# Four of nine token chunks in pairs with seven block products instead of eight (Strassen), weights from DRAM, and a cosine from one sine

## The chip, the cores and the metric

The kernel runs on one core of one Trainium2 chip. A core has five engines that run their own instruction streams side by side: PE (TensorE, matmuls), ACT (ScalarE), DVE (VectorE), POOL (GpSimd) and SP (SyncE), which here only issues DMA transfers. Engines wait for each other by semaphores. PE takes its operands from SBUF and writes into PSUM, which has eight banks of 512 fp32 columns; ACT and DVE read PSUM. The metric is the device time of one execution in microseconds, the median of the runs.

## What is computed

The reference, cut to its core (8 batches, 8 heads, 576 tokens, head size 64; 4608 tokens of width 512, inner width 2048):

```python
kv = np.einsum('bhsd,bhse->bhde', k, v)
out = np.einsum('bhsd,bhde->bhse', q, kv)
rms = np.sqrt(np.mean(out * out, axis=-1, keepdims=True) + 1e-06)
attn = out / rms * g_norm
x = attn.transpose(0, 2, 1, 3).reshape(B * S, H * D)   # 4608 x 512
h = x @ w_in                                           # first product, 512 x 2048
g = h * np.cos(h)
return (g @ w_out).astype(np.float32)                  # second product, 2048 x 512
```

## The kernel before

The 4608 tokens are cut into nine chunks of 512 (`CH`, `NCH`). For each chunk the attention part makes four tiles x of 128 features by 512 tokens (`NP` = 4, one tile for two heads). Then come 16 steps (`NJ`), one for each 128 of the inner width: the first product of step j adds four x tiles times a block of w_in into one PSUM bank (tile `bank`), `act_part` turns the bank into g = h cos h, and the second product (`stage2_part`) adds g times a block of w_out into four banks `acc`, one for each 128 tokens of the chunk.

Every fp32 operand is split into a high part in the matmul's own format (fp32r) and the rest (`xhi`/`xlo`, `ghi`/`glo`, and `w[:, 0]`/`w[:, 1]` of a weight). A product of two operands is three matmuls, high·high, low·high and high·low, so a step has 4 x 3 matmuls in the first product and as many in the second, all of 128 x 512.

`act_part` runs on ACT and DVE in turn: ki (ACT, the number of turns in h, rounded by the write to int32), r = h - ki C1 and r = r - ki C2 (DVE, twice), sine of r/2 and square (ACT, twice), (r - 0.5) h (DVE), then ghi (ACT) and glo (DVE). That makes g times -1/2, and the copy of `acc` to the output scales by -2.

`x_part` makes an x tile of chunks 2 to 8: DVE transposes q, ACT and DVE split it (`m`, `sg`), PE multiplies it with the split k-v product (`kv_w`) into two banks, ACT and DVE bring these together, then come square, transpose, reduce and a swap of rows (`part`, `swp`, `ms`), a power -1/2 on POOL (`rinv`), and the scaling with `gcol` (the norm's gain). x is last split into xhi and xlo. The attention of a chunk is done while an earlier chunk's steps run.

The weights arrive as 64-bit floats and are turned into split fp32 by `w_part` during the first two chunks; from then on all 32 blocks (`wi0` to `wi15`, `wo0` to `wo15`) stay in SBUF. At the start these same buffers hold k, v and q of the first two chunks.

The order of work on each engine is set by a planner in the kernel's Python code (`Order`): every part of the work is a generator that waits for events, takes buffer tokens (`t_bank` for PSUM banks, `t_slot`, `t_two`) and asks for time on an engine with a priority, mostly from `due(i)`, the time wanted for step i; a table of numbers (`haste`) moves single priorities. The instructions are pinned in the planned order, so on the chip each engine runs its own row, and waits where an input is late. All instructions are issued through one helper (line 207), so the profile's groups are told apart by tile names.

Of the kernel before, what the change touches and what calls it, by code (L numbers as in the profile page):

```python
# [19 lines left out]
P = 128  # L20
# [3 lines left out]

C1 = 6.28125
C2 = 2.0 * PI - C1

# [13 lines left out]
class Tokens:  # L41
    def __init__(self, n):
        self.free = [(0.0, i) for i in range(n)]
        self.waiters = []
# [7 lines left out]
class Order:  # L52
# [23 lines left out]
    def advance(self, proc, value):  # L76
        while True:
# [18 lines left out]
            else:  # L96
# [4 lines left out]
                t, value = heapq.heappop(tokens.free)  # L101
# [10 lines left out]
    def give(self, tokens, t, which=0):  # L112
        if tokens.waiters:
            _, _, proc = heapq.heappop(tokens.waiters)
            proc.t = max(proc.t, t)
            self.advance(proc, which)
        else:
            heapq.heappush(tokens.free, (t, which))
# [36 lines left out]
def tile_kernel(  # L155
# [73 lines left out]


# [24 lines left out]

    segments = [(0, 0, 4), (1, 0, 8), (0, 4, 16), (1, 8, 16)]
    segments += [(c, 0, NJ) for c in range(segments[-1][0] + 1, NCH)]
# [9 lines left out]
    STEP = 5.4  # L267

    def due(i):

        return 24.0 + STEP * i + 2.0 * min(i, 11)


    haste = {
# [9 lines left out]
        ("act", 16): 16.2, ("act", 29): 32.0, ("act", 35): 63.7, ("act", 4): -10, ("act", 5): -8.1,  # L284
        ("act", 8): 10.6, ("acc", 0): 28.7, ("acc", 1): 19.9, ("acc", 10): 20.7, ("acc", 13): 59.2,
        ("acc", 14): 44.4, ("acc", 18): 32.3, ("acc", 26): 10.6, ("acc", 28): 15.6, ("acc", 33): 25.2,
        ("acc", 46): 5.6, ("acc", 53): 6.8, ("acc", 8): 12.3, ("xd", 2, 0): -3.8, ("xd", 2, 2): -11.8,
        ("xd", 2, 3): -24.5, ("xd", 3, 0): -12.5,
# [50 lines left out]
    def load(us, prio, event, issue, wait=(), take=None):  # L339
        def part():  # L340
            if wait:
                yield "wait", wait
            if take:
                yield "take", take
# [6 lines left out]
    def load_g():  # L351
        pass
# [271 lines left out]
    def x_part(c, p, prio):  # L624
# [11 lines left out]
        for j, r in enumerate(rows):  # L636
            yield "run", [("ACT", act_us())], prio
            act.copy(out=qs[j][r], in_=qT[r])
            _, end = yield "run", dve_only(CH), prio
            dve.tensor_tensor(out=qs[j][rows[1 - j]], in0=qT[r], in1=qs[j][r].bitcast(F32), op=ALU.subtract)  # L640
# [16 lines left out]
        x_slot = yield "take", t_slot, prio  # L657
        x = slot_tile(x_slot)
# [39 lines left out]
        sched.give(t_slot, end, slot)  # L698
        yield "take", t_x, prio
# [58 lines left out]
    gates = [Event() for _ in steps]  # L758

    def window(c):  # L760

        first = last_step[c - 2] + 1
        return first, begin[c] - first

    def stage1_part(i):
# [3 lines left out]
        yield "wait", [w_done["wi", j]]  # L769
        yield "take", t_h  # L770
# [223 lines left out]
```

## Time and profile before

| what | value |
|---|---|
| median of 3 runs | 859.64 us (859.44 to 859.7) |
| profiled execution, first to last instruction (span) | 858.1 us |
| granted clock of PE, mean | 0.999 |
| instructions | 12178 |
| DMA | 59.51 MB, mean 69 GB/s |
| DMA in the first 60 us | 334 GB/s |

The span is what the profile covers; the device time of a run has a little more around it, 1.5 us by the median. In the rows of the profile an arrow reads "written tile <- read tiles", then come the shapes, "x" and the number of instructions, busy time in us, the mean of one in ns, and the time that the engine sat idle just before them with what ended it. PE's weight loads (PEld) overlap its matmuls. Rows of the timeline begin with the start in us and the length; rows of windows give a stretch and the busy time of each engine in it.

### The profile page before, as it was taken

The numbers are of one execution on the slowest core, as the hardware profiler recorded it, in microseconds if no ns is written. First come the engines' busy times: TensorE is split into PE (matmuls) and PEld (weight loads), VectorE is DVE, ScalarE is ACT, GpSimd is POOL, SyncE is SP. The second block draws the span as 40 slices with busy tenths as digits, with TensorE's granted clock in tenths as the row PEclk, the third lists the DMA queues.
The fourth block names the chain that finished last, engine by engine and source line by source line (L and its number), as shares of the span: only waits on it lengthen the run. The fifth ranks groups of instructions, "written<-read, shape, count | busy, mean of one in ns | idle before, by whom it ended". The sixth has DMA issues, their size and how long they took to land.

```text
span 858.1 us, 12178 instructions
## 1 busy us (share of the span) xinstructions
PE 848.1 (99%) x4496; PEld 701.5 (82%) x4496; DVE 651.0 (76%) x1053; ACT 556.2 (65%) x1059; POOL 103.6 (12%) x49
## 2 busy tenths in 40 slices
PE   8999999999999999999999999999999999999998
PEld 7678888888788888888888888888888888888886
DVE  4998988899987757885778667876777678864554
ACT  4888988666665656665666566756666666664443
POOL 3210000013121101110102101210112011110000
PEclk9999999999999999999999999999999999999999
DMA  9996021361304011301122020402000110010001
GB/s 306 323 321 216 2 86 37 101 194 33 104 15 116 5 63 24 111 12 39 45 66 63 3 73 13 121 4 62 13 13 14 49 25 1 2 45 4 1 1 49
DMA packets 104635, 59.51 MB, mean 69 GB/s; under 512 B 69632, under 2 KB 94976, under 8 KB 104576
## 3 DMA queue, kind: packets, MB, share of 16 engines
q1 hardware_dynamic: 104064, 58.02, 23.3%
q8 instruction: 35, 0.57, 0.3%
q10 hardware_dynamic: 512, 0.72, 0.2%
q14 instruction: 24, 0.20, 0.1%
HBM read 47.19 MB, written 11.53 MB: 68 GB/s over the span
## 4 chain that ended last, share of the span: by engine, by line
PE 95%; DVE 2%; POOL 1%; ACT 1%; DMA 1%; issue 0%; ACTq 0%; POOLq 0%; DVEq 0%
PE bank L207 49%; PE acc L207 45%; POOL rinv L207 1%; DVE r L207 1%; DMA gcol<-in_g_norm_dram 1%; DVE sg L207 0%; DVE ms L207 0%; ACT m L207 0%; ACT slot L207 0%; DVE xlo L207 0%; ACT r L207 0%; DVE m L207 0%; ACTq L207 0%; DVE wo L207 0%; ACT wo L207 0%
## 5 line engine op out<-in xcount | busy, mean ns | idle before, releaser
L207 PE MATMUL acc<-wo,ghi 128*128 128x512 f32 x1152 | 355.5, 390 | 0.0
L207 PE MATMUL bank<-xhi,wi 128*128 128x512 f32 x1088 | 337.1, 391 | 0.4 <-DVE wi L207 0.4
L207 PEld LDWEIGHTS acc<-wo,ghi 128*128 128x128 f32 x1152 | 215.6, 188 | 45.1 <-DVE slot L207 0.4
L207 ACT ACTIVATE r<-r 128x512 f32<-128x512 f32 x288 | 181.5, 631 | 94.6 <-DVE r L207 92.0
L207 PEld LDWEIGHTS bank<-xhi,wi 128*128 128x128 f32 x1088 | 202.4, 188 | 41.9 <-DVE wi L207 0.7
L207 PE MATMUL acc<-wo,glo 128*128 128x512 f32 x576 | 224.5, 390 | 0.3 <-DVE glo L207 0.3
L207 PE MATMUL bank<-xlo,wi 128*128 128x512 f32 x544 | 212.1, 390 | 0.1
L207 POOL TENSOR_TENSOR rinv<-ms,mhalf 128x16 f32<-128x16 f32 (+1 forms) x36 | 99.1, 2757 | 648.9 <-DVE ms L207 648.9
L207 DVE SCALAR_TENSOR_TENSOR r<-ki,bank 128x512 f32<-128x512 int32 x144 | 98.6, 685 | 72.3 <-ACT ki L207 70.8
L207 ACT ACTIVATE ki<-bank 128x512 int32<-128x512 f32 x144 | 85.6, 594 | 90.0 <-PE bank L207 86.4
L207 DVE SCALAR_TENSOR_TENSOR r<-r,bank 128x512 f32<-128x512 f32 x144 | 98.2, 682 | 55.1 <-ACT r L207 54.4
L207 PEld LDWEIGHTS acc<-wo,glo 128*128 128x128 f32 x576 | 108.1, 188 | 23.4 <-DVE glo L207 0.7
L207 PEld LDWEIGHTS bank<-xlo,wi 128*128 128x128 f32 x544 | 102.1, 188 | 21.9 <-DVE xlo L207 0.6
L207 ACT CAST ghi<-r 128x512 fp32r<-128x512 f32 x144 | 89.1, 620 | 43.5 <-DVE r L207 40.9
L207 DVE TENSOR_TENSOR glo<-r,ghi 128x512 fp32r<-128x512 f32 x144 | 98.9, 687 | 23.6 <-ACT ghi L207 21.3
L207 DVE SCALAR_TENSOR_TENSOR r<-ki,r 128x512 f32<-128x512 int32 x144 | 98.5, 684 | 1.2
L207 DVE TENSOR_TENSOR slot<-bank,slot 64x512 f32<-64x512 f32 x56 | 38.5, 688 | 19.1 <-ACT slot L207 18.1
L207 ACT COPY slot<-bank 64x512 f32<-64x512 f32 x56 | 32.5, 581 | 21.1 <-PE bank L207 20.2
L207 ACT ACTIVATE slot<-acc 128x512 f32<-128x512 f32 (+1 forms) x39 | 22.5, 592 | 9.6 <-PE acc L207 8.4
L207 ACT COPY swp<-part 32x16 f32<-32x16 f32 x112 | 22.6, 202 | 7.5 <-DVE part L207 5.8
L207 DVE STREAM_TRANSPOSE slot<-rinv 128x512 f32<-128x512 f32 x28 | 19.8, 705 | 4.1 <-POOL rinv L207 4.0
L207 DVE SCALAR_TENSOR_TENSOR sg<-sg,m 128x512 int32<-128x512 int32 x32 | 21.7, 685 | 0.3 <-ACT sg L207 0.3
(94 smaller groups left out, 573.3 us busy)
## 6 DMA issues: line engine op xcount, KB each, us to landing
out_dram<-slot SPq DMA_DIRECT2D x35, 256.0 KB, 2.0
wo<-in_moe_w_out_dram SPq DMA_DIRECT2D x16, 512.0 KB, 8.3
wi<-in_moe_w_in_dram SPq DMA_DIRECT2D x16, 512.0 KB, 9.4
m<-in_k_dram SPq DMA_DIRECT2D x24, 256.0 KB, 3.3
sg<-in_v_dram SPq DMA_DIRECT2D x24, 256.0 KB, 3.8
part<-slot SPq DMA_DIRECT2D x8, 256.0 KB, 5.3
slot<-part SPq DMA_DIRECT2D x8, 256.0 KB, 2.9
qb<-in_q_dram SPq DMA_DIRECT2D x32, 48.0 KB, 2.8
```

What stands on the lines that cost most here:

```text
L207: return lambda *a, **kw: tc.keep_in_program_order(f(*a, **kw))
```

## The change

**Seven products.** Chunks 0 to 4 (`PLAIN` = 5) keep their steps. Chunks 5 and 6, and 7 and 8, are taken as pairs. The x of a pair is seen as a 2 x 2 matrix of blocks (chunk by half of the features), and two blocks j = 2m, 2m+1 of w_in with their two halves as another. `quad_part` makes the four h tiles of a pair for two blocks in seven block products (A11, S1, S2, A12, S4, S3, A22; Strassen's scheme in Winograd's form) instead of eight. The sums of x (S1 to S4) are made by `cross_part` from the unsplit x tiles, and each of the seven operands is split anew; the sums of the weights are made once by `sums_part` on POOL and ACT during steps 40 to 79. Between products, ACT copies a bank to SBUF (`snap`), the next product adds on in the same bank, and DVE adds bank and copy (`add`).

**Weights from DRAM.** The split weights are written to DRAM (`keep_in`, `keep_out`, `sums_part`) from step 34 on, 56 pieces for the first product (`wq`) and 16 blocks for the second (`wod`). In the pairs they are loaded again, two pieces or one block of 512 KB at a time (`load_in` into buffers `wo8` to `wo11`, `load_out` into `wo12` to `wo15`). The other weight buffers become room for the seven operands (`wi0` to `wi13`), for copies (`wi14`, `wi15`) and for x and g tiles (`wo0` to `wo7`, and the former `xhi`, `xlo`, `r`).

**Second product.** In the pairs g is kept unsplit until `split_part` and `gather_part` take it, in units of one (chunk, j): 16 units of chunk 5 beside the first pair, 32 beside the second, the 16 of chunk 8 at the end.

**Cosine.** h comes out in turns, since 1/(2 pi) is put into `gcol`. Then cos h is the sine of 2 pi (h + 1/4 - round(h + 1/4)): ki (ACT), one subtraction (DVE), one sine (ACT), one product with h (DVE). The output is scaled by 2 pi.

**Engines and order.** Some additions and subtractions may go to POOL or DVE, whichever the planner finds free (`adders`). `haste` is another table, and `due` has another pace for the pairs.

The core of the diff:

```diff
-C1 = 6.28125
-C2 = 2.0 * PI - C1
+OUT_SCALE = 2.0 * PI
...
     def g_part():
         yield "wait", [g_in]
-        yield "run", [("ACT", 0.1)], -11.0
-        act.copy(out=gcol[D:2 * D, :], in_=gcol[0:D, :])
+        yield "run", [("ACT", 0.4)], -11.0
+        for r in (slice(D, 2 * D), slice(0, D)):
+            act.activation(out=gcol[r, :], in_=gcol[0:D, :], func=AF.Copy, scale=INV_2PI)
...
+    def adders(f=CH, late=0.4):
+        return [("POOL", 0.2 + f / 460, 0.0), ("DVE", dve_us(f), late)]
...
-        act.activation(out=ki, in_=h, func=AF.Copy, scale=INV_2PI)
+        act.activation(out=ki, in_=h, func=AF.Copy, bias=0.25)
...
-        dve.scalar_tensor_tensor(out=r, in0=ki, scalar=-C1, in1=h, op0=ALU.mult, op1=ALU.add)
+        dve.scalar_tensor_tensor(out=r, in0=h, scalar=0.25, in1=ki, op0=ALU.add, op1=ALU.subtract)
...
+        act.activation(out=r, in_=r, func=AF.Sin, scale=2.0 * PI)
-        dve.scalar_tensor_tensor(out=r, in0=ki, scalar=-C2, in1=r, op0=ALU.mult, op1=ALU.add)
-        act.activation(out=r, in_=r, func=AF.Sin, scale=0.5)
-        act.activation(out=r, in_=r, func=AF.Square)
-        dve.scalar_tensor_tensor(out=r, in0=r, scalar=0.5, in1=h, op0=ALU.subtract, op1=ALU.mult)
+        dve.tensor_tensor(out=r, in0=r, in1=h, op=ALU.mult)
...
+    def sums_part(m, prio):
+        yield "wait", [w_done["wi", 2 * m], w_done["wi", 2 * m + 1]]
...
+        for j, t in ((2 * m, even), (2 * m + 1, odd)):
+            w = w_split["wi", j].bitcast(F32)
+            pool.tensor_tensor(out=t, in0=w[:, 0], in1=w[:, 1], op=ALU.add)
...
+        pool.tensor_tensor(out=even, in0=odd, in1=even, op=ALU.subtract)
...
+        for t, places in ((even, (S1, A22)), (odd, (S3, S2))):
+            act.copy(out=hi, in_=t)
+            pool.tensor_tensor(out=t, in0=t, in1=hi.bitcast(F32), op=ALU.subtract)
+            for half, q in enumerate(places):
+                for n, part in enumerate((hi.bitcast(F32), t)):
+                    nc.sync.dma_start(out=wq[:, 7 * m + q, n], in_=part[:, half * WH:(half + 1) * WH])
...
+    def load_in():
+            slot = yield "take", t_win
+            w = wpool.tile([P, 2, 2, WH], F32R, name=f"wo{slot}")
+            nc.sync.dma_start(out=w.bitcast(F32), in_=wq[:, s:s + 2])
...
+        def product(q, bank, first, gate=None):
+            yield "wait", [win_in[s // 2]] + [cross_done[pair, q, k] for k in range(HK)]
+            for k in range(HK):
+                for i, (a, b) in enumerate(((0, 0), (1, 0), (0, 1))):
+                    pe.matmul(
+                        out=ps[bank], lhsT=w[:, s % 2, a, cols], rhs=x[:, b],
+                        start=(first and k == 0 and i == 0), stop=(k == HK - 1 and i == 2), skip_group_check=True)
...
+        end = yield from product(A11, b2, True, 0)
+        sched.spawn(snap("p1", b2, at(A11) - 8.0), end + 0.1)
+        end = yield from product(S1, b3, True)
+        sched.spawn(snap("p5", b3, at(S1) - 8.0), end + 0.1)
+        yield "wait", [done["p1"]]
+        end = yield from product(S2, b2, False, 1)
+        sched.spawn(snap("u2", b2, at(S2) - 8.0), end + 0.1)
+        end = yield from product(A12, b1, True)
+        yield "wait", [done["p5"]]
+        end = yield from product(S4, b3, False, 2)
+        yield "wait", [done["u2"]]
+        end = yield from product(S3, b2, False, 3)
+        yield "wait", [u3]
+        end = yield from product(A22, b2, False)
```

Three places in the order of instructions show what moved. Names carry a running number; a row stands for one instruction or, with "x3", for three alike.

On PE, at the entry into chunk 5, before: the last second products of chunk 4 (here that with `wo14`) are laced into the first step of chunk 5 (x times `wi0` into `bank3`):

```order
L207 MATMUL bank3_5098<-xhi_5070,wi0_448 128x512 x2
L207 MATMUL bank3_5098<-xlo_5071,wi0_448 128x512
L207 MATMUL acc0_4395<-wo14_1815,ghi_5153 128x512 x2
L207 MATMUL acc0_4395<-wo14_1815,glo_5154 128x512
L207 MATMUL acc1_4400<-wo14_1815,ghi_5153 128x512 x2
L207 MATMUL acc1_4400<-wo14_1815,glo_5154 128x512
L207 MATMUL acc2_4406<-wo14_1815,ghi_5153 128x512 x2
L207 MATMUL acc2_4406<-wo14_1815,glo_5154 128x512
L207 MATMUL acc3_4412<-wo14_1815,ghi_5153 128x512 x2
L207 MATMUL acc3_4412<-wo14_1815,glo_5154 128x512
```

On PE, the same entry now, from the last second product of chunk 4 (`wo15`): then come the products of the first quad, operands in `wi` buffers, weights in `wo8` to `wo10`; A11 stands further up in the row:

```order
L206 MATMUL acc3_4642<-wo15_1623,ghi_5416 128x512 x2
L206 MATMUL acc3_4642<-wo15_1623,glo_5417 128x512
L206 MATMUL bank0_5450<-wi2_5455,wo8_5254 128x512 x3
L206 MATMUL bank0_5450<-wi9_5564,wo8_5254 128x512 x3
L206 MATMUL bank3_5323<-wi4_5465,wo9_5318 128x512 x3
L206 MATMUL bank3_5323<-wi10_5576,wo9_5318 128x512 x3
L206 MATMUL bank1_5597<-wi3_5513,wo9_5318 128x512 x3
L206 MATMUL bank1_5597<-wi8_5584,wo9_5318 128x512 x3
L206 MATMUL bank0_5450<-wi5_5533,wo10_5344 128x512 x3
L206 MATMUL bank0_5450<-wi12_5604,wo10_5344 128x512 x3
L206 MATMUL bank3_5323<-wi6_5518,wo10_5344 128x512 x3
L206 MATMUL bank3_5323<-wi13_5598,wo10_5344 128x512 x3
```

S1, S2, A12, S4 and S3 follow each other without a second product between them, and `bank0` and `bank3` are each written a second time after two other products.

On ACT, the first instructions before (m and wo15 are parts of the attention of chunk 0, warm loads the sine's table):

```order
L207 DMA wi6_146<-in_k_dram 128x576
L207 DMA wo4_147<-in_v_dram 128x576
L207 ACT_TABLE_LOAD
L207 ACTIVATE warm_80<-warm_80 128x1
L207 DMA gcol_138<-in_g_norm_dram 64x1
L207 COPY gcol_138<-gcol_138 64x1
L207 COPY m_158<-bank0_152 128x512
L207 COPY m_169<-bank1_162 128x512
```

On ACT, the first instructions now:

```order
L206 ACT_TABLE_LOAD
L206 COPY m_177<-bank0_172 128x512
L206 DMA wi6_200<-in_k_dram 128x576
L206 DMA wo4_201<-in_v_dram 128x576
L206 ACT_TABLE_LOAD
L206 ACTIVATE warm_80<-warm_80 128x1
L206 DMA gcol_138<-in_g_norm_dram 64x1
L206 COPY wo15_158<-bank1_181 64x64 x2
L206 COPY wo15_158<-bank2_206 64x64 x2
L206 COPY m_243<-bank3_230 128x512
L206 ACTIVATE gcol_138<-gcol_138 64x1 x2
L206 ACTIVATE slot0_257<-acc3_245 128x512
```

The loads of k, v and g stand behind a copy that reads PE's first transpose, and a square (`slot0`) stands behind the two instructions on `gcol`.

On DVE, at the entry into chunk 5, before: the steps' instructions on r and the last splits (xlo, glo):

```order
L207 TENSOR_TENSOR xlo_5071<-slot1_4729,xhi_5070 128x512
L207 TENSOR_TENSOR xlo_5075<-slot0_4952,xhi_5074 128x512
L207 SCALAR_TENSOR_TENSOR r_5088<-ki_5055,bank2_4998 128x512
L207 SCALAR_TENSOR_TENSOR r_5088<-ki_5055,r_5088 128x512
L207 SCALAR_TENSOR_TENSOR r_5108<-ki_5102,bank0_5043 128x512
L207 SCALAR_TENSOR_TENSOR r_5088<-r_5088,bank2_4998 128x512
L207 SCALAR_TENSOR_TENSOR r_5108<-ki_5102,r_5108 128x512
L207 TENSOR_TENSOR glo_5154<-r_5088,ghi_5153 128x512
```

On DVE, the same entry now: the last x tile (`wo1`) is scaled between sums and splits of the products' operands (`slot3` and `slot4` are sums, `wi` their low parts):

```order
L206 STREAM_TRANSPOSE slot0_5515<-rinv_5451 128x512
L206 TENSOR_TENSOR wi3_5513<-xhi_4749,wi3_5513 128x512
L206 TENSOR_TENSOR wi6_5518<-wo0_4646,wi6_5518 128x512
L206 TENSOR_TENSOR wi7_5524<-wo1_4680,wi7_5524 128x512
L206 SCALAR_TENSOR_TENSOR wo1_4680<-wo1_4680,gcol_138,slot0_5515 128x512
L206 TENSOR_TENSOR kv_w_79<-bank2_5467,kv_w_79 64x4x64
L206 TENSOR_TENSOR slot3_5540<-wo0_4646,wo1_4680 128x512
L206 TENSOR_TENSOR sg_5464<-qT_5461,sg_5464 64x512
L206 TENSOR_TENSOR wi9_5564<-slot3_5540,wi9_5564 128x512
```

Between `rinv` and the operand of S1 (`wi9`) there are now nine instructions in DVE's row.

More of the change, by code (lines that the diff above doesn't have):

```diff
@@ new lines, in split_part @@
+    def split_part():
+        for u, (c, j) in enumerate(units):
+            prio = due_unit(u) - 4.0 + put_off("split", u)
+            yield "wait", [g_ready[c, j]]
+            yield "take", t_g, prio
+            r, held = g_raw[c, j]
+            yield "run", [("ACT", act_us())], prio
+            ghi = ew.tile([P, CH], F32R, name="ghi")
+            glo = ew.tile([P, CH], F32R, name="glo")
+            act.copy(out=ghi, in_=r)
+            e, end = yield "run", adders(CH, 0.0), prio
+            adder(e).tensor_tensor(out=glo, in0=r, in1=ghi.bitcast(F32), op=ALU.subtract)
+            sched.give(t_store, end, held)
+            g_pairs[c, j] = ghi, glo
+            sched.fire(g_split[c, j], end)
```

386 lines of the change are left out of this document (351 added, 35 removed), and 12 rows, old and new, of the table haste.

## The prediction

> **What bounds the kernel now.** I read the page first, then the groups with shapes kept apart, then a stretch of the timeline, then windows of one chunk each, and last the start of the timeline.
>
> ```profile
> span 858.1 us, 12178 instructions
> PE 848.1 (99%) x4496; PEld 701.5 (82%) x4496; DVE 651.0 (76%) x1053; ACT 556.2 (65%) x1059; POOL 103.6 (12%) x49
> PE 95%; DVE 2%; POOL 1%; ACT 1%; DMA 1%; issue 0%; ACTq 0%; POOLq 0%; DVEq 0%
> ```
>
> TensorE is busy in 99% of the span and is 95% of the chain that ended last. "Busy" is modelled, so I look at the rate:
>
> ```profile
> 606.40 0.61 PE L207 MATMUL acc<-wo,ghi 128*128 128x512 f32 x2
> 606.85 0.39 PE L207 MATMUL acc<-wo,glo 128*128 128x512 f32 x1
> 607.08 0.61 PE L207 MATMUL acc<-wo,ghi 128*128 128x512 f32 x2
> 607.53 0.39 PE L207 MATMUL acc<-wo,glo 128*128 128x512 f32 x1
> 607.76 0.61 PE L207 MATMUL acc<-wo,ghi 128*128 128x512 f32 x2
> ```
>
> Three matmuls start every 0.68 us (606.40, 607.08, 607.76): 0.2267 us each, whatever the listed 0.39. Now one chunk at a time, from one first product to the same one of the next chunk:
>
> ```profile
> 395.85:487.84 91.99, 91.99 (x482) 76.52 (x481) 68.56 (x110) 58.24 (x112) 11.92 (x4) 1.00 0.19 49
> 580.04:672.56 92.52, 92.52 (x481) 76.83 (x481) 68.95 (x110) 58.68 (x113) 11.91 (x4) 1.00 0.10 24
> ```
>
> The columns are length, busy time of PE, weight loads, DVE, ACT, POOL, then clock, DMA share and GB/s. 16 steps of 24 matmuls are 384 x 0.2267 = 87.0 us of the 92.0; the other 5.0 are the attention matmuls (8 of 512 columns, 1.8, and k-v products, some 3.1). There is no hole: DVE (75%) and ACT (63%) have reserve, and the clock is full. So in these chunks a matmul removed is 0.2267 us won, and DVE or ACT work removed is worth nothing by itself.
>
> **The products (the gain).** Per pair of chunks, eight quads of seven products replace 32 steps of first product. A product is 2 x 3 matmuls, a quad 42 instead of 48. Over 16 quads 96 matmuls go: 96 x 0.2267 = 21.8 us, all on the path that sets the end. The second product (1728 matmuls) and the attention matmuls stay. Weights are now taken from other buffers, still one load of 128 columns per matmul, so the rate stays. Against the span 858.1 this gives 836.3; the median of the runs, 859.64, lies 1.5 above the span, so 837.9 in device time.
>
> **The cosine.** Per tile one DVE and one ACT instruction go:
>
> ```profile
> L207 ACT ACTIVATE r<-r 128x512 f32<-128x512 f32 x288 | 181.5, 631 | 94.6 <-DVE r L207 92.0
> L207 DVE SCALAR_TENSOR_TENSOR r<-ki,bank 128x512 f32<-128x512 int32 x144 | 98.6, 685 | 72.3 <-ACT ki L207 70.8
> L207 DVE SCALAR_TENSOR_TENSOR r<-ki,r 128x512 f32<-128x512 int32 x144 | 98.5, 684 | 1.2
> L207 DVE TENSOR_TENSOR glo<-r,ghi 128x512 fp32r<-128x512 f32 x144 | 98.9, 687 | 23.6 <-ACT ghi L207 21.3
> ```
>
> That is 144 x 0.684 = 98.5 us of DVE and 144 x 0.631 = 90.9 us of ACT. Both lie beside TensorE: gain zero on the path, but it is what pays for the rest.
>
> **What is added.** DVE: 48 additions that finish the products and 28 more sums and splits of x, less 37 that the order puts on POOL: 105 fewer in all. ACT: 48 copies out of PSUM, 12 more splits, 16 casts of weight sums: 68 fewer in all. POOL: 64 instructions for the weight sums and those 37. They cost nothing on the path as long as each stage has room, so I count the fullest one. Between the first product of the first pair and the first of the second, the order has 551 matmuls, about 118 us at the rates above, 174 instructions on DVE and 178 on ACT: it holds the attention of chunks 7 and 8 too. At the page's means (651.0/1053 = 0.618 and 556.2/1059 = 0.525, overlaps included) DVE takes 107.5 us, 91%, and ACT 93, 79%. At the 0.685 of a full tile DVE would take 119, that is 101%. So here the cover is thin, though units of second product are in store for PE. Bounds 0 and 12 us; I take 1.5, near the lower end, since the 0.618 includes the mix.
>
> POOL has not yet done such work. Its nearest rows:
>
> ```profile
> masks.py:199 POOL TENSOR_SCALAR_AFFINE_SELECT ident<-ident 128x128 f32<-128x128 f32 x1 | 0.3, 292 | 0.1
> masks.py:197 POOL MEMSET ident<- 128x128 f32 x1 | 0.2, 199 | 0.0
> L207 POOL MEMSET kv_w<- 128x1024 f32 x2 | 1.8, 951 | 0.0
> ```
>
> A write alone costs 0.84 ns a column (752 ns over 896 columns) and 0.09 us fixed; one read and a write 1.6 ns. A sum of two tiles of 512 columns then lies between 0.5 and some 1.8 us; I take 1.2, above the row with one read. The pow rows (2.90 us for 16 columns, below) are a function per element and no price for a subtraction. The weight sums are 8 x (5 x 1.2 + 3 x 0.65) = 64 us on a POOL that was idle for 80 of every 92 us.
>
> **Entry into a pair.** The order puts the last attention matmuls of chunk 6 inside the last step of chunk 4; the product with S1 needs what follows from them. The chain from there is made of these rows:
>
> ```profile
> L207 ACT COPY slot<-bank 64x512 f32<-64x512 f32 x56 | 32.5, 581 | 21.1 <-PE bank L207 20.2
> L207 DVE TENSOR_TENSOR slot<-bank,slot 64x512 f32<-64x512 f32 x56 | 38.5, 688 | 19.1 <-ACT slot L207 18.1
> L207 ACT ACTIVATE slot<-slot 128x512 f32<-128x512 f32 x28 | 17.6, 628 | 4.6 <-DVE slot L207 4.0
> L207 DVE STREAM_TRANSPOSE qT<-slot 128x512 f32<-128x512 f32 x28 | 19.8, 706 | 0.9 <-ACT slot L207 0.7
> L207 DVE TENSOR_REDUCE part<-qT 128x16 f32<-128x512 f32 x28 | 19.0, 677 | 0.4
> L207 ACT COPY swp<-part 32x16 f32<-32x16 f32 x112 | 22.6, 202 | 7.5 <-DVE part L207 5.8
> L207 DVE SCALAR_TENSOR_TENSOR ms<-part,swp 128x16 f32<-128x16 f32 x28 | 4.8, 170 | 4.1 <-ACT swp L207 4.0
> ```
>
> Two evacuations 2 x (0.58 + 0.69), square 0.63, transpose and reduce 1.38, four swaps 0.81, 0.17, pow some 3.1 (rows below), five DVE instructions of the order 3.5, then sum, cast and subtraction with one more DVE instruction between 2.5: 14.6, with hand-overs about 15.4 us. PE has 72 matmuls and a batch of k-v products until then: 16.3 + 3.1 = 19.4. Slack 4, on a DVE that also serves the last steps: bounds 0 and 5, I take 1.5. The second entry has 93 matmuls, 21 us: nothing.
>
> **The start.** ACT's first copy now stands ahead of its own loads of k, v and g:
>
> ```profile
> 0.73 0.46 ACTq L207 DMA_DIRECT2D wi<-in_k_dram  x1
> 1.21 0.49 ACTq L207 DMA_DIRECT2D wo<-in_v_dram  x1
> 1.74 1.28 ACT L207 ACT_TABLE_LOAD   x1 [1.74 <-issue]
> 1.80 0.53 ACTq L207 DMA_DIRECT2D gcol<-in_g_norm_dram  x1
> 4.86 0.63 PE L207 MATMUL bank<-ident,wi 128*128 128x128 f32 x4
> 7.49 0.19 ACT L207 COPY gcol<-gcol 64x1 f32<-64x1 f32 x1 [4.25 <-DMA gcol<-in_g_norm_dram]
> 10.60 0.60 ACT L207 ACTIVATE slot<-acc 128x512 f32<-128x512 f32 x1 [0.34 <-PE acc L207]
> 27.42 0.50 PE L207 MATMUL bank<-xhi,wi 128*128 128x512 f32 x1 [0.40 <-DVE wi L207]
> ```
>
> That copy waits for the transpose (to 5.49) and the loads behind it go out at about 6.1, 6.6 and 7.1 instead of 0.73, 1.21 and 1.80. With the 5.7 us that g took, it lands near 12.8; behind it in ACT's row stands the first square, at 10.60 before: 2.5 us late. A second table load (1.28 us) fits into that wait. But the first step waited for its weights (DVE wi), and those are now the 11th issue on SP instead of the 16th, and the order begins with two of the four x tiles. Bounds -3 and +2.5; I take +1.
>
> Sum: 859.64 - 21.8 + 1.5 + 1.5 + 1 = 841.9.
>
> **Transfers.** 120 loads of 512 KB come back from DRAM, 62.9 MB, in the last 340 us or so of PE work: 185 GB/s, on SP's queue. Rows:
>
> ```profile
> 55.00:60.00 5.00, 5.00 (x24) 4.11 (x23) 5.00 (x10) 4.15 (x9) 0.00 (x0) 1.00 1.01 347
> wo<-in_moe_w_out_dram SPq DMA_DIRECT2D x16, 512.0 KB, 8.3
> slot<-part SPq DMA_DIRECT2D x8, 256.0 KB, 2.9
> ```
>
> The queue moved 347 GB/s, so the rate is there. Latency: a buffer is free after a unit of second product (2.72 us) and wanted three units, 8.2 us, later. Even the 8.3 us of the crowded start would cost some 0.5 us per four units, 1.5 us in the tail; the 2.9 for 256 KB in a less crowded stage speaks for none. I add nothing. The stores, 23 MB, go out from step 34 on beside 49 GB/s: hidden.
>
> **Rivals.** *POOL and DVE in each other's way.* Two rows of pow, with what DVE did in them:
>
> ```profile
> 183.20 2.90 POOL L207 TENSOR_TENSOR rinv<-ms,mhalf 128x16 f32<-128x16 f32 x1 [130.72 <-DVE ms L207]
> 200.94 3.33 POOL L207 TENSOR_TENSOR rinv<-ms,mhalf 128x16 f32<-128x16 f32 x1 [14.83 <-DVE ms L207]
> 200.82 0.69 DVE L207 TENSOR_TENSOR m<-qT,m 64x512 fp32r<-64x512 f32 x1
> 202.39 0.69 DVE L207 TENSOR_TENSOR sg<-qT,sg 64x512 fp32r<-64x512 f32 x1 [0.16 <-ACT sg L207]
> 184.17 0.68 DVE L207 SCALAR_TENSOR_TENSOR r<-ki,bank 128x512 f32<-128x512 int32 x1
> ```
>
> Beside DVE instructions with two inputs in SBUF (200.82, 202.39) the pow took 0.43 us longer than beside one that reads a PSUM bank (184.17); DVE itself was not slowed. If each of the 16 full or half tiles that POOL gets in the first pair held such a DVE instruction for its 1.2 us, DVE would need 107.5 + 19.2 = 126.7 us against PE's 118: 9 us more, 851. Chance 0.18. [...]
>
> *Slower: the loads bind.* 62.9 MB must come in 340 + 21.8 = 362 us to be no worse than before, so below 174 GB/s the change loses; at 165 GB/s the stage lasts 381 us and the time is 879. Loads wait in order in one queue for buffers, which speaks for it, 347 GB/s against. Chance 0.05.
>
> *The gain is eaten inside the quads.* Each quad returns four times to a PSUM bank after a copy or addition (0.58 or 0.69 us): 64 returns. If each held PE 0.34 us, the 21.8 us are gone and the time is 859.6. The order leaves 1.36 us of other matmuls in the shortest gaps, 2.72 or more in most. Chance 0.03.
>
> *Better.* The start gains the 3 us and nothing stalls: 835. Chance 0.12.
>
> **How the numbers follow.** The forecast, 842 with its own range 837.5 to 847, has 0.62. Up from it lie 851 (0.18), 859.6 (0.03), 879 (0.05), below 835 (0.12). From 835 to 853 leaves out half of the "better" case, a third of the POOL case and the two dear ones: 2 in 10. A measurement tells about 0.2% (1.7 us) from no change: faster 0.62 + 0.18 + 0.12 = 0.92, same 0.03, slower 0.05.
>
> **What would show it.** Three matmuls every 0.68 us also in the quads; 96 fewer; idle time ahead of PE's products of at most a few us in sum, most at the first product with S1. DVE near 590 us, ACT near 515, POOL near 220. If DVE's mean for subtractions of SBUF tiles rises above 0.69 while POOL works, the first rival is right; if PE or its weight loads wait for a DMA, the second; if for copies out of PSUM, the third. I am wrong if the clock falls below 1.00 or if PE waits for POOL's sums.

## The result and the profile after

| what | before | after |
|---|---|---|
| median of 4 runs each, one chip | 859.56 us (859.44 to 859.7) | 852.97 us (852.87 to 854.03) |
| ratio, 95% interval | | 0.9923 [0.9911, 0.9936] |
| span of the profiled execution | 858.1 us | 851.2 us |
| granted clock of PE, mean | 0.999 | 0.995 |

The change gains 6.6 us, where 17.6 were forecast; the span falls by 6.9. The busy times on the page after, and its row of shares of the chain that ended last:

```profile
PE 830.2 (98%) x4400; PEld 686.0 (81%) x4400; DVE 614.3 (72%) x947; ACT 512.0 (60%) x993; POOL 233.2 (27%) x151
PE 85%; DVE 7%; ACT 2%; issue 2%; POOL 2%; DMA 2%; SPq 1%; ACTq 0%; DVEq 0%; POOLq 0%
```

The 96 matmuls are gone (4400 against 4496). At 0.2267 us each that is 21.8 us, so with the span 6.9 us shorter, 14.9 us were lost elsewhere. PE's share of the chain fell from 95% to 85%: there are now waits. The list of PE's waits from 60 us on (before: one, of 0.3 us):

```profile
PE bank L206 <- DVE wi L206: 2.3, 2, 1.7
PE bank L206 <- ACT wi L206: 1.4, 1, 1.4
PE bank L206 <- DVE r L206: 1.2, 1, 1.2
PE bank L206 <- DVE xlo L206: 0.7, 1, 0.7
PE bank L206 <- DVE sg L206: 0.5, 1, 0.5
```

Together 6.1 us, 5.8 more than before. The tile wi is here an operand of the products of a pair. xlo holds an x tile of the second pair: at 615.5 us PE waits until DVE has added a bank of the attention to it. None of the waits is for a DMA or for one of ACT's copies out of PSUM.

How much of the 14.9 us belongs to the start shows in the matmuls that PE got through in the first 100 us, before and after (the "x" behind PE's busy time):

```profile
0.00:100.00 100.00, 94.08 (x733) 76.41 (x734) 83.35 (x149) 75.87 (x153) 18.63 (x21) 1.00 0.78 250
0.00:100.00 100.00, 89.03 (x704) 73.97 (x705) 74.77 (x134) 71.66 (x146) 17.86 (x21) 0.97 1.00 331
```

All 29 that are missing are of 512 columns (248 against 277; the other 456 are alike). So the start lost 29 x 0.2267 = 6.6 us, and 8.3 us were lost behind 100 us, 5.8 of them in the listed waits.

The timeline of the start, issues on ACT's queue first (before, g was issued at 1.80, the first square stood at 10.60 and the first step at 26.52, its first full row at 27.42):

```profile
7.12 0.39 ACTq L206 DMA_DIRECT2D wi<-in_k_dram  x1
8.48 0.33 ACTq L206 DMA_DIRECT2D wo<-in_v_dram  x1
9.95 0.53 ACTq L206 DMA_DIRECT2D gcol<-in_g_norm_dram  x1
15.90 0.43 ACT L206 ACTIVATE gcol<-gcol 64x1 f32<-64x1 f32 x2 [3.84 <-DMA gcol<-in_g_norm_dram]
16.24 1.05 ACT L206 ACTIVATE slot<-acc 128x512 f32<-128x512 f32 x2
20.36 0.63 PE L206 MATMUL acc<-ident,r 128*128 128x128 f32 x4 [4.27 <-DVE r L206]
35.08 0.71 PE L206 MATMUL bank<-xhi,wi 128*128 128x512 f32 x2
```

g is issued 8 us later than before and ACT waits 3.84 us for it; the first square stands behind it, PE waits 4.27 us for the tile that follows, and the first step begins 8.6 us later; 2 of these are made up in the steps behind it, by the count of matmuls. Part of the loss is not waiting at all. Stretches of 2 us of the same start, the third column from the end being the granted clock:

```profile
20.00:22.00 2.00, 1.64 (x24) 1.50 (x26) 1.08 (x3) 0.93 (x2) 1.10 (x1) 0.73 1.08 260
22.00:24.00 2.00, 2.00 (x27) 1.88 (x24) 2.00 (x5) 1.12 (x5) 0.00 (x0) 0.50 1.11 308
24.00:26.00 2.00, 2.00 (x18) 2.00 (x18) 1.04 (x2) 1.38 (x3) 0.00 (x0) 0.91 1.04 340
30.00:32.00 2.00, 1.30 (x16) 1.09 (x18) 1.67 (x4) 1.84 (x4) 1.53 (x1) 0.79 1.11 256
32.00:34.00 2.00, 2.00 (x35) 1.47 (x32) 2.00 (x4) 1.14 (x6) 0.00 (x0) 0.50 1.03 295
34.00:36.00 2.00, 2.00 (x12) 1.87 (x13) 1.59 (x4) 1.50 (x4) 0.00 (x0) 0.85 1.01 354
```

The clock is halved twice, from 20.9 to 24.3 and from 31.2 to 34.6 us, each time behind a stretch in which PE stood. One spell costs (0.27 + 0.50 + 0.09) x 2 = 1.7 us of full clock, both 3.4 at most. In before it was 1.00 in every stretch from 8 to 60 us.

Last, the entry into the first pair. In the timeline, DVE and POOL work side by side on SBUF tiles. PE does the first half of the product with S1 at 509.76 and then waits for the operand of the second half, first for its high part (ACT), then for its low part (DVE):

```profile
504.79 3.47 DVE L206 TENSOR_TENSOR wi<-wo,wi 128x512 fp32r<-128x512 f32 x2
508.19 1.77 DVE L206 SCALAR_TENSOR_TENSOR wo<-wo,gcol,slot 128x512 f32<-128x512 f32 x1
504.29 1.73 POOL L206 TENSOR_TENSOR xhi<-xhi,slot 128x512 f32<-128x512 f32 x1
506.10 1.62 POOL L206 TENSOR_TENSOR m<-qT,m 64x512 fp32r<-64x512 f32 x1
507.79 1.62 POOL L206 TENSOR_TENSOR wi<-xhi,wi 128x512 fp32r<-128x512 f32 x1
509.76 0.84 PE L206 MATMUL bank<-wi,wo 128*128 128x512 f32 x3
512.01 0.73 PE L206 MATMUL bank<-wi,wo 128*128 128x512 f32 x2 [1.41 <-ACT wi L206]
513.36 6.66 PE L206 MATMUL bank<-wi,wo 128*128 128x512 f32 x25 [0.61 <-DVE wi L206]
```

Three DVE instructions of forms that take 0.68 (wi<-wo,wi) and 0.74 us (wo<-wo,gcol,slot) where they are shortest in this kernel take 1.74, 1.74 and 1.77 here, while POOL works almost without a break from 503.04 to 509.41. The second entry shows the same, a wait of 1.7 us for the low part that DVE makes here:

```profile
660.75 1.75 DVE L206 TENSOR_TENSOR wi<-slot,wi 128x512 fp32r<-128x512 f32 x1
660.23 1.71 POOL L206 TENSOR_TENSOR wi<-xlo,wi 128x512 fp32r<-128x512 f32 x1
```

**The theory:** (a) the start lost some 7 us to g's late load, about half of it through the halved clock; (b) POOL's sums hold up DVE instructions that read two SBUF tiles, and this lengthens the chains into the pairs. The rivals: other moves in the start (k and v, the order of x tiles); a DVE row too long at the entries by its count alone; a gain that came from the cosine.

### The profile page after: what moved, and what is told of

It reads as the page before. It is cut to its first block, busy times and chain, and to the rows that moved or that the text cites. A ratio compares the mean times of both kernels' runs of the same rounds, so it can differ in the third digit from the quotient of the medians.

```text
span 851.2 us, 12582 instructions
## 1 busy us (share of the span) xinstructions
PE 830.2 (98%) x4400; PEld 686.0 (81%) x4400; DVE 614.3 (72%) x947; ACT 512.0 (60%) x993; POOL 233.2 (27%) x151
## 4 chain that ended last, share of the span: by engine, by line
PE 85%; DVE 7%; ACT 2%; issue 2%; POOL 2%; DMA 2%; SPq 1%; ACTq 0%; DVEq 0%; POOLq 0%
PE bank L206 44%; PE acc L206 40%; POOL rinv L206 1%; DVE glo L206 1%; DVE wi L206 1%; DVE wo L206 1%; DVE slot L206 1%; DMA gcol<-in_g_norm_dram 1%; DVE xlo L206 1%; DMA wi<-in_q_dram 1%; DVE qT L206 1%; DVE r L206 1%; ACT wi L206 1%; ACT ki L206 0%; SPq L415 0%
## 5 line engine op out<-in xcount | busy, mean ns | idle before, releaser
L206 PE MATMUL bank<-xhi,wi 128*128 128x512 f32 x576 | 178.3, 391 | 0.0
L206 PE MATMUL bank<-wi,wo 128*128 128x512 f32 (+2 forms) x756 | 165.7, 375 | 4.5 <-DVE wi L206 2.3
L206 PEld LDWEIGHTS bank<-wi,wo 128*128 128x128 f32 (+2 forms) x756 | 128.5, 185 | 34.2 <-DVE wi L206 4.1
L206 PEld LDWEIGHTS bank<-xhi,wi 128*128 128x128 f32 x576 | 107.3, 188 | 22.0
L206 PE MATMUL bank<-xlo,wi 128*128 128x512 f32 x288 | 112.2, 390 | 0.0
L206 DVE SCALAR_TENSOR_TENSOR r<-bank,ki 128x512 f32<-128x512 f32 x82 | 56.3, 686 | 35.0 <-ACT ki L206 34.0
L206 ACT CAST ghi<-r 128x512 fp32r<-128x512 f32 x89 | 55.2, 620 | 38.9 <-PE acc L206 29.8
L206 ACT ACTIVATE r<-r 128x512 f32<-128x512 f32 x89 | 55.9, 630 | 17.9 <-DVE r L206 17.0
L206 DVE TENSOR_TENSOR r<-r,bank 128x512 f32<-128x512 f32 x82 | 55.7, 681 | 10.9 <-ACT r L206 10.0
L206 PEld LDWEIGHTS bank<-xlo,wi 128*128 128x128 f32 x288 | 54.0, 188 | 11.4
```

The source lines that it names most:

```text
L206: return lambda *a, **kw: tc.keep_in_program_order(f(*a, **kw))
```

## The experiments

**The load of g at the head.**

```diff
     gcol = const.tile([P, 1], F32, name="gcol")
+    act.dma_start(out=gcol[0:D, :], in_=g_norm.rearrange("(d o) -> d o", o=1))
...
                 act.activation(out=warm, in_=warm, func=AF.Sin)
-                act.dma_start(out=gcol[0:D, :], in_=g_norm.rearrange("(d o) -> d o", o=1))
```

> The changed kernel with one edit: the load of g is issued by ACT at the head of its row, ahead of the copy of the first x tile; the loads of k and v stay behind that copy. Theory A (the start is lost to g): in the changed kernel g was issued at 9.95 us and landed at 15.90, with the first square right behind it at 16.24 (before: 1.80, 7.49 and 10.60). With g early the square waits for its own operands only, the first step (35.08 against 26.52) comes 4 to 7 us earlier, and the time falls from 853.0 to about 847.5 (846 to 849.5). Theory B (the start is lost to k and v, which are issued at 7.12 and 8.48, or to the changed order of x parts and weights): the first step moves by less than 1.5 us and the time stays at 852 to 853.

Measured: 847.3 us, ratio to before 0.9846 [0.9827, 0.9865], 5.7 below the changed kernel (which was measured in another round than the experiments; the kernel before, measured in every round, had medians of 859.56 to 859.87). Its timeline:

```profile
0.73 0.56 ACTq L206 DMA_DIRECT2D gcol<-in_g_norm_dram  x1
12.07 0.60 ACT L206 ACTIVATE slot<-acc 128x512 f32<-128x512 f32 x1 [0.49 <-PE acc L206]
29.41 0.71 PE L206 MATMUL bank<-xhi,wi 128*128 128x512 f32 x2
```

The square now waits 0.49 us for PE and for nothing else, the first step comes 5.7 us earlier, and by 100 us PE has done 729 matmuls, 25 more than in the changed kernel (5.7 us): theory A. One spell of half clock, from 25.4 to 28.8 us, is left in this execution. The waits from 60 us on are the same 6.1 us as in the changed kernel.

**k, v and g at the head.**

```diff
-            load(..., [kv_in[c, p]] + ([] if c or p else [g_in]), kv_loads_front(c, p, ...))
+            issue = kv_loads_front(c, p, ...)
+            if not c and not p:
+                issue()
+            load(..., [kv_in[c, p]] + ([] if c or p else [g_in]), issue if c or p else lambda: None)
```

> The changed kernel with the loads of k, v and g of the first tile all issued at the head of ACT's row, as in the kernel before; everything else keeps its order. Theory A (the start is lost to g alone): as the run with only g early, 846 to 849, within 1 us of it. Theory B (k and v count too): 1.5 to 4 us faster than the run with only g early. Theory C (the new order of x parts and weights is what costs): still 851.5 to 853. The first two say that the lag against the kernel before is gone from 60 us on, and that the granted clock between 20 and 40 us is back at 1.00.

Measured: 848.05 us (846.11 to 850.99), 0.9858 [0.9833, 0.9883]: as the run before within its spread, which goes with the mean granted clock of the executions (846.11 at 1.000, 850.99 at 0.992). In the profiled execution, span 844.2, no spell of half clock is left and the first step stands at 27.96. So k and v add nothing that can be told from the clock, and with the clock full this execution is 851.2 - 844.2 = 7.0 us shorter than the changed kernel's, of which at most 3.4 is the clock. The first step is still 1.4 us later than before (27.96 against 26.52), but by 100 us PE has done 735 matmuls, two more than before: nothing of the start's loss is left.

**Filling PE's idle.** That the idle itself halves the clock was tested apart:

```diff
         _, end = yield "run", [("PE", 0.5)], prio
+        if c == 0 and p < 2:
+            spare = ps_o.tile([P, DM], F32, name=("acc3", "acc2")[p])
+            for _ in range((24, 64)[p]):
+                pe.matmul(out=spare[:, 0:P], lhsT=zeros, rhs=zeros, start=True, stop=True)
         for a in range(NTT):
             pe.transpose(out=ps[:, a * P:(a + 1) * P], in_=x[:, a * P:(a + 1) * P], identity=ident)
```

> The changed kernel with 88 small matmuls of zeros added at the start, 64 where PE waited 4.27 us for the first x tile and 24 where it waited 1.78 us; nothing reads them, the late load of g stays. In the changed kernel the granted clock was 0.50 from about 20.9 to 24.3 us and from 31.6 to 35.0 us, each time some 5 us after an idle stretch began. Theory A (the idle itself lowers the clock, and that is half of the start's loss): the clock stays at 1.00 up to 60 us, each spell gives back about 1.7 us, and the time falls by 2.5 to 3.5 us, to 849.5 to 850.5. Theory B (the spells overlap with waits for g's chain, or don't hang on PE's idle): 852 to 853.5.

Measured: 850.92 us, 0.9897 [0.9883, 0.991], 2.05 below the changed kernel, though 88 matmuls were added and g is as late as there. Stretches of 2 us:

```profile
12.00:14.00 2.00, 2.00 (x15) 2.00 (x15) 0.00 (x0) 0.00 (x0) 0.00 (x0) 0.76 1.04 401
14.00:16.00 2.00, 2.00 (x27) 1.67 (x27) 0.00 (x0) 0.27 (x2) 0.00 (x0) 0.50 0.95 332
22.00:24.00 2.00, 2.00 (x35) 1.93 (x30) 1.79 (x4) 1.93 (x7) 0.00 (x0) 1.00 1.08 244
32.00:34.00 2.00, 2.00 (x14) 1.73 (x13) 2.00 (x5) 1.97 (x4) 0.00 (x0) 1.00 1.09 261
510.00:512.00 2.00, 1.39 (x5) 1.04 (x5) 1.86 (x2) 1.74 (x4) 1.92 (x3) 0.85 0.86 268
512.00:514.00 2.00, 2.00 (x6) 1.52 (x6) 2.00 (x2) 1.42 (x3) 1.55 (x1) 0.50 0.85 312
```

Both spells of the changed kernel are gone, and two others have come: one at 13 us, behind an idle of 1.8 us that was not filled, and one from 511.4 to 514.8 us at the entry into the first pair, behind the same waits of 1.41 and 0.61 us that left the clock at 1.00 in the changed kernel. The first step comes 2.6 us earlier (32.49 against 35.08), and by 100 us PE has done 715 matmuls without the added ones, 11 more than in the changed kernel, 2.5 us. The spell at the entry takes 0.8 of that back, so that the span falls by 1.7 (851.2 to 849.5). So A holds in kind: with the idle of the start filled, the clock stays at 1.00 from 18 to 36 us, where it had been at 0.50 for twice 3.4 us in the changed kernel. In size it falls a little short, and the same waits at the entry lowered the clock in this execution and not in that of the changed kernel.

**POOL writes instead of reading.** The 37 sums and subtractions that the order gives to POOL in the x parts and the combinations are done on 16 columns, and the rest of each of these tiles is left at zero:

```diff
+    class WriteOnly:
+        def tensor_tensor(self, out, in0, in1, op):
+            pool.tensor_tensor(out=out[:, 0:16], in0=in0[:, 0:16], in1=in1[:, 0:16], op=op)
+            for _ in range(2):
+                pool.memset(out[:, 16:CH].bitcast(F32), 0.0)
...
     def adder(e):
-        return pool if e == "POOL" else dve
+        return WriteOnly() if e == "POOL" else dve
```

> The changed kernel with the same order; each sum or subtraction of two SBUF tiles that the order gives to POOL in the x parts and in the combinations of a pair (37 in all) is computed on 16 columns only, and the other 496 columns are written with zeros by two POOL memsets, so those operands are wrong beyond column 16. POOL's weight sums stay. POOL stays about as long at work at these places, but hardly reads SBUF there. Theory A (POOL's reading blocks DVE's instructions with two SBUF inputs, which lengthens the chains into the pairs): the mean of DVE's sums of two SBUF tiles at the entries falls from 1.41 (wi<-wo,wi) and 1.35 (wi<-slot,wi) to about 0.69 us, PE's waits at 512 us (3.1 in sum) and 662 us (1.7 and what is in its 19 matmuls) shrink to under 1 us each, and the time falls by 4 to 7 us, to 846 to 849. Theory B (the chains are too long by the count of their instructions, the lock is beside them): the waits stay, 851.5 to 853.5.

Measured: 849.03 us, 0.9862 [0.984, 0.9884], 3.9 below the changed kernel. Its groups of DVE:

```profile
L206 DVE TENSOR_TENSOR wi<-slot,wi 128x512 fp32r<-128x512 f32 x7 | 4.7, 681 | 1.6 <-ACT wi L206 1.6
L206 DVE TENSOR_TENSOR wi<-wo,wi 128x512 fp32r<-128x512 f32 x3 | 2.0, 694 | 0.2 <-ACT wi L206 0.2
```

and its list of PE's waits from 60 us on:

```profile
PE bank L206 <- DVE r L206: 1.2, 1, 1.2
PE bank L206 <- DVE xlo L206: 0.7, 1, 0.7
```

The first two groups in the changed kernel:

```profile
L206 DVE TENSOR_TENSOR wi<-slot,wi 128x512 fp32r<-128x512 f32 x7 | 9.4, 1353 | 0.5 <-ACT wi L206 0.4
L206 DVE TENSOR_TENSOR wi<-wo,wi 128x512 fp32r<-128x512 f32 x3 | 4.2, 1409 | 0.0
```

Without the reading they take half, and every wait at an entry goes: 6.1 to 1.9 us. The span falls by 3.0, and that hides a part: this execution's start came out worse (first step 36.79 against 35.08, with the clock down to 0.50 from 18.9 to 25.7 us and again from 32.5; 691 matmuls by 100 us against 704, so 2.9 us). Behind 100 us it is therefore 6.0 us shorter, of the 8.3 lost there. A part of this may be POOL's own work, which also got shorter (226.0 us busy against 233.2, 0.2 us for each of the 37); that was not separated. What stays long is glo<-r,ghi (0.758 us in the mean against 0.687 in the kernel before), which stands beside POOL's weight sums: in the changed kernel it took up to 1.82 us between 230 and 420 us, where these are made, and 0.69 at most from 60 to 200 and from 420 to 500 us. Those sums were left as they are, and taking them off POOL was not tried.

**The same 37 on DVE.**

```diff
     def adder(e):
-        return pool if e == "POOL" else dve
+        return dve
```

> The changed kernel with the same order, the 37 sums and subtractions that POOL had got in the x parts and the combinations put on DVE at the place where they stood in the order; POOL keeps the weight sums. With those 37 hardly reading, PE's waits after 60 us had fallen from 6.4 to 1.3 us and DVE's busy time from 614 to 598. Theory A (POOL's 1.3 to 1.8 us of reading holds DVE up by as much as or more than the 0.69 us that DVE needs for the sum itself): DVE near 598 + 37 x 0.67 = 623 us, PE's waits after 60 us fall to between 2 and 4 us, the time to 849 to 851.5. Theory B (DVE's row at the entries is too long by its count): the waits grow above 6.4 us and the time to 853.5 to 857.

In the expectation the waits are counted by the distances of matmul starts (6.4, 1.3); the list of waits has 6.1 and 1.9 for the same two kernels. Measured: 850.75 us, 0.9905 [0.9891, 0.9919], 2.2 below the changed kernel; waits 4.5 us by the list, just above A's bound of 4. Its start is like the changed kernel's (705 matmuls by 100 us), so nearly all of the gain lies behind it. DVE is busy 620.2 us against 614.3: 37 more instructions for 5.9 us, 0.16 us each, so a sum on POOL had saved DVE almost nothing. Both theories hold a part: of the 6.0 us behind 100 us that vanish without the reading, 2.0 also vanish when DVE does the sums itself, and 4.0 come back with the work on DVE's row.

**Both mended.** The first edit of this section and the last one together.

> Both edits together: g's load at the head of ACT's row, and the 37 additions on DVE. Theory A (start and entries are two separate losses, each its own cause): the gains add, 847.3 - 3 = 844.3, between 842.5 and 846. Rival (with the start mended the work arrives earlier and the entries wait longer, or the second edit is worth nothing): 846.5 to 848.

Measured: 844.38 us, 0.9826 [0.9813, 0.984], as the sum had it. The profiled execution agrees: 731 matmuls by 100 us against 704 are 6.1 us, and behind 100 us it is 2.0 us shorter, as with the second edit alone. So the losses at the start and at the entries are separate. This is the fastest version measured, 8.6 us below the changed kernel. With k and v at the head as well:

> The loads of k, v and g at the head of ACT's row and the 37 additions on DVE. With g alone at the head the two edits gave 844.38. Theory A (after g, what is left of the start is small): 843 to 845.5, and executions differ by the granted clock of the start. Theory B (k and v still cost): 840.5 to 842.5.

Measured: 844.96 us (844.26 to 847.44), 0.9828 [0.9812, 0.9843]: no difference that can be told from the spread, so k and v hardly mattered.

**POOL reading in the kernel before.** Here POOL's reading alone is put into a kernel that has nothing of the change.

```diff
+    scr = const.tile([P, 192], F32, name="scr")
...
+        if 40 <= i < 120:
+            w = w_split["wi", 15].bitcast(F32)[:, :, 0:192]
+            for _ in range(7):
+                pool.tensor_tensor(out=scr, in0=w[:, 0], in1=w[:, 1], op=ALU.subtract)
```

> The kernel before, with seven sums of 192 columns on POOL added to each of the steps 40 to 119; they read two tiles of SBUF and write a scratch tile, and nobody waits for them. Theory A (POOL's reading and DVE's instructions with two SBUF inputs exclude each other): DVE's glo<-r,ghi, 0.687 us before, takes 0.8 to 1.1 us in the mean in these steps, and r<-ki,bank (one input in PSUM) stays at 0.685. PE has its cover, so the time grows by 0 to 6 us. Theory B (no such lock; the long DVE instructions of the changed kernel have another cause): both stay at 0.69 us, the time at 859.6 within 1.

And its control, with `for _ in range(15): pool.memset(scr, 0.0)` in the same place:

> The kernel before, with fifteen POOL memsets of 192 columns added to each of the steps 40 to 119, which only write. With seven sums there, reading two tiles, POOL was busy 518 us, glo<-r,ghi went from 0.687 to 0.812 and r<-ki,r from 0.684 to 0.792, while the forms with one input in PSUM stayed at 0.68; the time rose to 912.7, since POOL's own pow came late. Theory A (reading is what excludes): POOL about as busy, 400 us or more, all four DVE forms at 0.68 to 0.70; if pow comes late the time still rises, to anything between 860 and 910. Theory B (any POOL work in SBUF slows DVE): glo<-r,ghi and r<-ki,r at 0.75 or more.

Measured: 912.68 us, 1.0619 [1.0605, 1.0634], with reading; 863.34 us in the one execution of the control, too few to tell its time from that of the kernel before; its rows are what counts. The groups with reading:

```profile
L207 POOL TENSOR_TENSOR scr<-wi 128x192 f32<-128x192 f32 x560 | 416.1, 743 | 42.2
L207 DVE TENSOR_TENSOR glo<-r,ghi 128x512 fp32r<-128x512 f32 x144 | 116.9, 812 | 22.7 <-ACT ghi L207 20.6
L207 DVE SCALAR_TENSOR_TENSOR r<-ki,r 128x512 f32<-128x512 int32 x144 | 114.0, 792 | 1.2
L207 DVE SCALAR_TENSOR_TENSOR r<-ki,bank 128x512 f32<-128x512 int32 x144 | 98.0, 680 | 49.6 <-ACT ki L207 48.8
```

and the groups of the control:

```profile
L207 POOL MEMSET scr<- 128x192 f32 x1200 | 310.1, 258 | 67.9
L207 DVE TENSOR_TENSOR glo<-r,ghi 128x512 fp32r<-128x512 f32 x144 | 98.9, 687 | 23.6 <-ACT ghi L207 21.3
L207 DVE SCALAR_TENSOR_TENSOR r<-ki,r 128x512 f32<-128x512 int32 x144 | 98.6, 685 | 1.2
```

With POOL reading, the two forms with both inputs in SBUF took 0.812 and 0.792 us in the mean, against 0.687 and 0.684 in the kernel before; r<-ki,bank, which reads one of its two from PSUM, took 0.680 against 0.685. With POOL only writing they took 0.687, 0.685 and 0.685. 80 of the 144 tiles are in the loaded steps, so if the whole rise lies there, glo<-r,ghi takes 0.687 + (0.812 - 0.687) x 144/80 = 0.91 us in them. The time of the first of these runs was far above the 0 to 6 us that I allowed: 7 x 0.743 = 5.2 us fill POOL's row in each step of 5.4 us, POOL is 44% of its chain, and the pow that the attention needs came late. That is work queueing on POOL, and not DVE being held up. The control's memsets took 310 us in all, less than the load of the sums (416), but DVE's busy time stayed at 651.4 us (651.0 before).

**The cosine alone**, in the kernel before with its order:

```diff
...
-        dve.scalar_tensor_tensor(out=r, in0=ki, scalar=-C1, in1=h, op0=ALU.mult, op1=ALU.add)
-        dve.scalar_tensor_tensor(out=r, in0=ki, scalar=-C2, in1=r, op0=ALU.mult, op1=ALU.add)
-        act.activation(out=r, in_=r, func=AF.Sin, scale=0.5)
-        act.activation(out=r, in_=r, func=AF.Square)
-        dve.scalar_tensor_tensor(out=r, in0=r, scalar=0.5, in1=h, op0=ALU.subtract, op1=ALU.mult)
+        dve.scalar_tensor_tensor(out=r, in0=h, scalar=0.25, in1=ki, op0=ALU.add, op1=ALU.subtract)
+        act.activation(out=r, in_=r, func=AF.Sin, scale=2.0 * PI)
+        dve.tensor_tensor(out=r, in0=r, in1=h, op=ALU.mult)
```

> The kernel before with the cosine by one sine only, and the order of the kernel before: one DVE and one ACT instruction less in each of the 144 tiles, PE's work and every load the same. Theory A (DVE and ACT lie beside PE): DVE falls from 651 to about 552 us, ACT from 556 to about 465, and the time stays at 859.6, within 1 us. Theory B (a part of the 6.6 us gained comes from the cosine, so that the pairs of chunks gave still less): 853 to 857.

Measured: 859.0 us against 859.71, 0.9991 [0.9979, 1.0003]: no change that can be told. DVE is busy 566.7 us and ACT 474.6 (651.0 and 556.2 before), so 84 us of DVE and 82 us of ACT left the kernel, and nothing of it reached the time. DVE's fall is less than the 99 us that I had from the means of its rows.

**One pair only** (`PLAIN = 7` in the version with both mended):

> The same two edits as in the run of 844.38 (g's load at the head, 37 additions on DVE), and only chunks 7 and 8 as a pair: chunks 5 and 6 go through the plain first product, so 48 matmuls of 512 columns are saved, not 96. Theory A (each pair saves its 48 x 0.2267 = 10.9 us, less 1 to 3 us at its entry; the start's rest of 1 to 3 us does not hang on the pairs): 859.7 - 10.9 + 2 to 5 = 851 to 854. Theory B (a pair saves less than its matmuls also in the steady stretch, or the first pair bears nearly all of the loss): 846 to 849 or above 856.

Measured: 856.63 us, 0.9967 [0.9956, 0.9977], outside A's range and within B's "above 856". The span is 854.8, that is 7.6 above 858.1 - 10.9. Its single entry in the timeline:

```profile
686.46 13.84 PE L206 MATMUL bank<-wi,wo 128*128 128x512 f32 x47 [3.25 <-ACT wi L206]
```

and the stretches of 2 us around it:

```profile
686.00:688.00 2.00, 1.54 (x4) 1.21 (x5) 2.00 (x4) 1.78 (x4) 0.00 (x0) 0.50 1.00 385
692.00:694.00 2.00, 2.00 (x8) 1.56 (x8) 0.69 (x1) 0.22 (x1) 0.00 (x0) 0.84 0.04 10
```

PE waits 3.25 us, and then the clock is halved until 692.6, which costs (0.50 + 0.50 + 0.50 + 0.16) x 2 = 3.3 us at most (the stretches from 688 and 690 are at 0.50 too), and 2.6 by the distances of the matmuls' starts, as it began while PE still stood. The start cost nothing: by 100 us PE has done 737 matmuls, four more than before, so 8.5 us were lost behind it. The wait and the spell are 5.9 to 6.6 of them, two waits of 1.2 and 0.6 us at 341 and 628 us another 1.7. So it was not B's mechanism: the loss stands at the entry, while a pair saves its 48 matmuls to within 1 us, and loses at its entry more than the 1 to 3 us that I had allowed. The planner made another order for this kernel, so why its entry waits longer than those of 844.38 (1.4 us at most) was not taken apart.

## Why the prediction was right or wrong

**The products, -21.8: right.** 96 matmuls fewer, no wait inside a quad for a copy or an addition, or for loads; what was lost was lost elsewhere.

**The cosine, 0 on the path: right**, shown alone in the kernel before.

**The fullest stage, +1.5: about right.** Between the entries, the waits are 0.5 (for sg) and 0.7 (for xlo). DVE did not become the bound: 614.3 us busy against some 590 forecast.

**The entries, +1.5 and "nothing": this step failed.** The first waits 1.4 + 0.6 us by the list, 3.1 by the starts; the second, which had "21 us" of cover, waits 1.7. Wrong was the price of a DVE instruction in the chain, taken from rows without a busy POOL (0.69 us where it is now 1.35 to 1.41 in the mean), and with it the slack. Behind 100 us 8.3 us were lost, where the entries and the fullest stage had 3.0 together; 6.0 of them go when POOL hardly reads. Most of the other 2.3 are the waits that stay then, 0.7 us at 615 and 1.2 at 348 us, where no term of mine was; their cause was not taken apart.

**The start, +1 with bounds -3 and +2.5: this step failed by as much.** I had ACT's loads go out at 6.1, 6.6 and 7.1 behind its first copy; they went out at 7.12, 8.48 and 9.95, 1.4 to 1.5 us apart instead of 0.5, with a table load of 1.28 us ahead of the last. Why they stood so far apart was not taken apart. g landed at 15.9 instead of 12.8, and the square was late by 5.6 us instead of 2.5. The bound had no term for what a standing PE does to its clock, up to 3.4 us, though a clock below 1.00 was named as a sign of being wrong. The start lost 6.6 us, and all of it comes back with the loads at the head.

The sum: 6.6 us in the start where 1 was forecast, 8.3 behind it where 3.0 were: the 14.9 us lost. That 852.97 lies just inside the wide range of 835 to 853 owes nothing to these terms; the forecast's own range ended at 847.

**The rival POOL against DVE, 851 at 0.18:** its time is near the one measured by luck. Its sign came, a mean of DVE above 0.69 us (1.35 and 1.41 in the two rows at the entries), and it goes with POOL's reading: in the kernel before, glo<-r,ghi took 0.812 us in the mean beside POOL's sums against 0.687 beside its memsets. Its price did not come: I had it make DVE the bound of the fullest stage for 9 us. That was an estimate, 16 POOL tiles that each hold a DVE instruction for 1.2 us, and no run shows that sum. At the first entry three DVE instructions took 1.0 to 1.1 us more than at their shortest, and in all POOL's reading costs up to 6.0 us, mostly where a chain leads into a pair; nearly half of the loss is the start, on which the rival had nothing to say. The two rows of pow were no evidence as I read them, since beside the short one, too, stood a DVE instruction with two SBUF inputs:

```profile
185.37 0.68 DVE L207 SCALAR_TENSOR_TENSOR r<-ki,r 128x512 f32<-128x512 int32 x1
```

What was lacking was a row in which DVE takes longer beside POOL.

**The rivals of the loads and of the quads' returns: rightly small.** The page's rows for the blocks of the second and the first product, and PE's list without a DMA, decide it:

```profile
wo<-wod SPq DMA_DIRECT2D x64, 512.0 KB, 3.4
wo<-wq SPq DMA_DIRECT2D x56, 512.0 KB, 4.2
```

3.4 and 4.2 us to land, against the 8.2 us allowed.

## What to carry to other kernels

A load that an early instruction needs must not stand in an engine's row behind a compute instruction that waits: price a moved load by everything that its queue does ahead of it (here g went out at 9.95 us instead of 1.80), and allow for more than the length of the matmul engine's first waits, since its clock may follow (here two spells at 0.50, 3.4 us of full clock at most). How late the first step begins is not yet the loss: count the work done by a time well behind it. Work given to an idle engine is not free room where it makes another's instructions longer, as POOL's sums did (DVE's from 0.69 to as much as 1.82 us): one row of the victim beside the culprit, or a run that only adds the culprit, prices it. And when freed engine time lies beside the bound, as the cosine's did, put it to use only where a chain into the bound is not made longer by it.

## What the runs showed of the hardware

- When PE stood for 3.25 to 4.5 us (4.27 at 16 us in the changed kernel, 3.25 at the entry of the single pair, some 4.5 in the start of the run in which POOL writes), or in several shorter waits close together (0.88 and 1.78 us from 27 us on in the changed kernel), its granted clock fell to 0.50 within some 2.2 to 5.0 us of the idle's begin, for 3.4 us (both spells of the changed kernel) or 6.8 us (from 685.8 us with one pair). Such a spell costs up to 1.7 or 3.4 us. A single wait of 1.7 us in a busy stretch left the clock at 1.00 (at 662 us in the changed kernel). The same waits went either way: 1.41 and 0.61 us at the first entry left the clock at 1.00 in the changed kernel and halved it in the run with the filled gaps, and so did a gap of 1.7 to 1.8 us at 11 us. What decides between the two, the runs do not show.
- A POOL sum of two SBUF tiles of 128 x 512 took 1.27 us at best and up to 1.80 beside DVE in the changed kernel; the DVE instructions of that size with two SBUF inputs beside it went from 0.69 to as much as 1.82 us. Both engines lost time.
